# Gated linear attention followed by a squared-ReLU MoE layer: head-pair packing, one activation table and a new tracing order for the MoE

## The chip, the cores and the metric

The kernel runs on one core of one Trainium2 chip. The metric is the device time of one execution in microseconds (us). Engines are named as in the profile: PE (TensorE matmul), PEld (TensorE weight load, overlapping PE), DVE (VectorE), ACT (ScalarE), POOL (GpSimd) and SP (SyncE, which issues the DMAs here). The kernel before took 289.77 us, the median of three runs (289.43 to 291.96).

## The reference, cut to what matters

```python
# q, k, v, alpha: (4 batches, 8 heads, 768 tokens, 48), float32; alpha in 0.8..1.0
for t in range(S):                                    # gated linear attention (GLA)
    state = alpha[:, :, t, :, None] * state + einsum('bhd,bhe->bhde', k[:, :, t], v[:, :, t])
    y[:, :, t] = einsum('bhd,bhde->bhe', q[:, :, t], state)
x = y.transpose(0, 2, 1, 3).reshape(3072, 384)
h = x @ w_in                                          # 384 x 2048 ("MoE", first half)
r = maximum(h, 0); g = r * r
out = g @ w_out                                       # 2048 x 384 ("MoE", second half)
```

Both kernels do the GLA in 24 chunks of 128 tokens. Within a chunk, the running product of alpha becomes exp of a cumulative sum of ln(alpha); q is multiplied by it, k is divided by it, and the rest is matmul. State passes from chunk to chunk. The MoE part of a group of tokens can run as soon as the group's chunks have left the GLA.

## The kernel before

This is one GLA chunk, cut to what the change and the argument touch.

```python
nc.scalar.activation(L, at, AF.Ln)                     # ACT: one table
nc.tensor.matmul(pm, lhsT=utri_b2, rhs=L, ...)         # PE: cumulative sum
for h in range(H):                                     # PE: 8 column sums
    nc.tensor.matmul(state_ps[0:D, HD + h:HD + h + 1], lhsT=L[:, h*D:(h+1)*D], rhs=ones_col, ...)
nc.scalar.activation(A, pm, AF.Exp)                    # ACT: another table
nc.scalar.activation(Ainv, pm, AF.Exp, scale=-1.0)
nc.scalar.copy(vb, vt)                                 # ACT
nc.vector.tensor_mul(qki[:, :, 0, 0:D], qt, A)         # DVE (cut)
nc.vector.tensor_mul(qki[:, :, 1, 0:D], kt, Ainv)      # DVE (cut)
for h in range(H):                                     # q and k of one head share a transpose
    nc.tensor.transpose(pqkT[:, h, :], qki[:, h, :, :], ident_bf)
nc.vector.tensor_copy(qT[0:D, :, :], pqkT[0:D, :, :])
nc.scalar.copy(kT[0:D, :, :], pqkT[64:64 + D, :, :])   # ACT, 1,024 elements a lane
for r in range(2):
    for hh in range(4):                                # scores, 128 rows of which 48 hold data
        nc.tensor.matmul(ps[:, hh, :], lhsT=kT[:, h, :], rhs=qT[:, h, :], ...)
    nc.vector.tensor_mul(sm[:, r*4:(r+1)*4, :], ps, utri_b.to_broadcast([P, 4, P]))
# ... output matmuls, xn, three transposes pxT, copy into xT_big (ACT), new state ...
```

The main loop places half of a 256-token MoE group (eight `ph` groups of three matmuls, then one `po` tile of sixteen) after every chunk. Half of the ReLUs are on ACT, half on DVE:

```python
gla_chunk(...)
if sc >= 2:
    moe1_slice(sc // 2 - 1, range(8 * i, 8 * i + 8))
if sc >= 6:
    moe2_slice(jj // 2, [jj % 2])
```

## Time and profile before

| what | before |
|---|---|
| median time, runs beside the kernel after | 289.6 us (289.11 to 291.96, 4 runs) |
| busy: PE, ACT, DVE, POOL | 220.0, 196.0, 170.5, 63.7 us of 287.6 |
| ACT table loads | 49, of 1,283 ns: 63 us |
| copy of a chunk's result into `xT_big`: sixth, last | 72.51, 259.56 us |

The copy into `xT_big` is the last step of a chunk's GLA output, and its start times are a clock for progress. From the sixth to the last they are (259.56 - 72.51) / 18 = 10.4 us apart.

From the profile page of the kernel before, these are the busy times, the forty slices of PE and ACT (each digit is tenths of a slice), and the shares of the chain that ended last:

```profile
PE 220.0 (76%) x2176; PEld 150.8 (52%) x2176; DVE 170.5 (59%) x382; ACT 196.0 (68%) x353; POOL 63.7 (22%) x108
PE   0334887867787868889869789988867989999884
ACT  2777677687879988773984878796765696633100
ACT 39%; PE 34%; issue 12%; DVE 9%; DMA 4%; SPq 1%; ACTq 0%; DVEq 0%
```

No engine is full on average, but the chain passes through ACT more often than through PE. From the groups of the same page (busy us, mean ns of one; then idle time of the engine before them and who ended it), the reason:

```profile
L145 DVE TENSOR_TENSOR qki_s<-qt,A 128x384 bf16<-128x384 f32 x24 | 13.3, 556 | 36.7 <-ACT A L135 36.7
L122 ACT ACT_TABLE_LOAD x24 | 30.8, 1283 | 0.4
L162 ACT COPY kT_s<-pqkT 48x1024 bf16<-48x1024 bf16 x24 | 24.2, 1009 | 9.4 <-DVE qT_s L161 9.0
L135 ACT ACT_TABLE_LOAD x21 | 26.9, 1283 | 0.3
```

DVE waited 36.7 us in all for the exp.

### The profile page before, as it was taken

How to read it: one execution, taken by the hardware profiler on the slowest of the kernel's cores; microseconds unless marked ns; L12 is line 12 of the kernel's file. 1: busy time of each engine (PE TensorE's matmuls, PEld its weight loads, DVE VectorE, ACT ScalarE, POOL GpSimd, SP SyncE). 2: the span in 40 equal slices, each digit the busy share in tenths (PEclk: the TensorE clock that was granted, in tenths of full speed). 3: DMA queues.
4: the chain of work that ended last, by engine and by line, in shares of the span. 5: the costliest groups of instructions: out<-in, count | busy, mean ns of one | idle time of the engine just before them, and what ended most of it. 6: DMA issues, size and time to landing. Idle time of an engine off the chain costs nothing.

```text
span 287.6 us, 5744 instructions
## 1 busy us (share of the span) xinstructions
PE 220.0 (76%) x2176; PEld 150.8 (52%) x2176; DVE 170.5 (59%) x382; ACT 196.0 (68%) x353; POOL 63.7 (22%) x108
## 2 busy tenths in 40 slices
PE   0334887867787868889869789988867989999884
PEld 0223654644454555656546556655545656666542
DVE  5145566768466666646567558656665757785500
ACT  2777677687879988773984878796765696633100
POOL 3000022222111223122123113221222212333300
PEclk9999998999979999797999999999979999999999
DMA  8999899600776395823633625653440200000111
GB/s 158 248 229 243 200 239 277 136 2 0 141 107 138 84 181 76 158 68 72 136 74 69 137 55 113 112 120 76 109 82 30 55 32 30 27 2 28 55 57 55
DMA packets 107036, 30.26 MB, mean 105 GB/s; under 512 B 100352, under 2 KB 105472, under 8 KB 107008
## 3 DMA queue, kind: packets, MB, share of 16 engines
q1 hardware_dynamic: 107008, 29.89, 48.3%
q8 instruction: 17, 0.28, 0.4%
q14 instruction: 11, 0.09, 0.1%
HBM read 25.17 MB, written 4.72 MB: 104 GB/s over the span
## 4 chain that ended last, share of the span: by engine, by line
ACT 39%; PE 34%; issue 12%; DVE 9%; DMA 4%; SPq 1%; ACTq 0%; DVEq 0%
PE ph L209 13%; PE po L228 11%; ACT L135 6%; ACT r L217 6%; ACT L122 5%; ACT L L122 4%; ACT A L135 4%; PE sc L170 3%; PE pqkT L158 3%; ACT kT_s L162 3%; ACT xT_big L189 2%; ACT state_b L201 2%; DMA w_out_f<-in_moe_w_out_dram 2%; DVE gT_big L218 2%; ACT vb L142 2%
## 5 line engine op out<-in xcount | busy, mean ns | idle before, releaser
L209 PE MATMUL ph<-xT_big,w_in_b 128*128 128x256 bf16 x576 | 94.4, 288 | 25.5 <-ACT r L217 14.7
L221 POOL TENSOR_TENSOR gT_big<-r 128x256 bf16<-128x256 bf16 x96 | 61.2, 637 | 206.2 <-DVE r L220 206.2
L228 PE MATMUL po<-w_out_b,gT_big 128*128 128x384 bf16 x384 | 85.8, 331 | 3.4 <-DVE ob L238 2.1
L209 PEld LDWEIGHTS <-w_in_b 128*128 128x128 bf16 x576 | 55.3, 102 | 44.6 <-issue 33.4
L217 ACT ACTIVATE r<-ph 128x256 bf16<-128x256 f32 x96 | 36.5, 380 | 35.6 <-PE ph L209 33.5
L218 DVE TENSOR_TENSOR gT_big<-r 128x256 bf16<-128x256 bf16 x96 | 31.7, 330 | 32.9 <-ACT r L217 30.1
L228 PEld LDWEIGHTS <-gT_big 128*128 128x128 bf16 x384 | 36.7, 99 | 19.8 <-issue 6.5
L220 DVE TENSOR_SCALAR r<-ph 128x256 bf16<-128x256 f32 x96 | 39.9, 415 | 4.6 <-PE ph L209 4.5
L172 DVE TENSOR_TENSOR sm<-sc,utri_b 128x512 bf16<-128x512 f32 x48 | 33.0, 688 | 14.4 <-PE sc L170 14.2
L145 DVE TENSOR_TENSOR qki_s<-qt,A 128x384 bf16<-128x384 f32 x24 | 13.3, 556 | 36.7 <-ACT A L135 36.7
L122 ACT ACT_TABLE_LOAD x24 | 30.8, 1283 | 0.4
L162 ACT COPY kT_s<-pqkT 48x1024 bf16<-48x1024 bf16 x24 | 24.2, 1009 | 9.4 <-DVE qT_s L161 9.0
L135 ACT ACT_TABLE_LOAD x21 | 26.9, 1283 | 0.3
L170 PEld LDWEIGHTS <-kT_s 128*128 128x128 bf16 x192 | 14.4, 104 | 23.2 <-ACT kT_s L162 11.8
L170 PE MATMUL sc<-qT_s,kT_s 128*128 128x128 bf16 x192 | 20.5, 234 | 7.0 <-ACT kT_s L162 5.6
L142 ACT CAST vb<-vt 128x384 bf16<-128x384 f32 x24 | 12.2, 509 | 17.0 <-PE sc L181 12.1
L161 DVE COPY qT_s<-pqkT 48x1024 bf16<-48x1024 bf16 x24 | 16.3, 679 | 7.1 <-PE pqkT L158 6.9
L158 PE MATMUL pqkT<-ident_bf,qki_s 128*128 128x128 bf16 x192 | 17.5, 243 | 3.8 <-DVE qki_s L150 3.8
L158 PEld LDWEIGHTS <-qki_s 128*128 128x128 bf16 x192 | 13.5, 109 | 9.0 <-DVE qki_s L150 8.3
L127 PE MATMUL state_ps<-ones_col,L 128*48 128x1 bf16 x192 | 9.6, 168 | 8.9 <-ACT L L122 8.7
L127 PEld LDWEIGHTS <-L 128*48 128x48 bf16 x192 | 7.4, 105 | 16.6 <-ACT L L122 8.7
L125 PE MATMUL pm<-L,utri_b_104 128*128 128x384 bf16 x24 | 8.6, 358 | 9.8 <-ACT L L122 9.8
(41 smaller groups left out, 218.9 us busy)
## 6 DMA issues: line engine op xcount, KB each, us to landing
qt<-in_q_dram SPq DMA_DIRECT2D x24, 192.0 KB, 3.5
kt<-in_k_dram SPq DMA_DIRECT2D x24, 192.0 KB, 4.0
vt<-in_v_dram SPq DMA_DIRECT2D x24, 192.0 KB, 4.3
at<-in_alpha_dram SPq DMA_DIRECT2D x24, 192.0 KB, 3.9
out_dram<-ob SPq DMA_DIRECT2D x24, 192.0 KB, 1.9
w_in_f<-in_moe_w_in_dram SPq DMA_DIRECT2D x4, 768.0 KB, 6.3
w_out_f<-in_moe_w_out_dram SPq DMA_DIRECT2D x4, 768.0 KB, 7.2
```

Of the source, the lines that this page charges most:

```text
L122: nc.scalar.activation(L, at, AF.Ln)
L135: nc.scalar.activation(A, pm, AF.Exp)
L158: nc.tensor.transpose(pqkT[:, h, :], qki[:, h, :, :], ident_bf)
L162: nc.scalar.copy(kT[0:D, :, :], pqkT[64:64 + D, :, :])
L170: nc.tensor.matmul(ps[:, hh, :], lhsT=kT[:, h, :], rhs=qT[:, h, :], start=True, stop=True)
L172: nc.vector.tensor_mul(sm[:, r * 4:(r + 1) * 4, :], ps, utri_b.to_broadcast([P, 4, P]))
L209: nc.tensor.matmul(ph, lhsT=w_in_b[:, j, f * P:(f + 1) * P], rhs=xT_big[:, j, t0:t0 + TG], start=(j == 0), stop=(j == KT - 1),)
L217: nc.scalar.activation(r, ph, AF.Relu)
L218: nc.vector.tensor_mul(gT_big[:, f, g % 3, :], r, r)
L220: nc.vector.tensor_single_scalar(r, ph, 0.0, ALU.max)
L221: nc.gpsimd.tensor_mul(gT_big[:, f, g % 3, :], r, r)
L228: nc.tensor.matmul(po, lhsT=gT_big[:, kf, g % 3, tt * P:(tt + 1) * P], rhs=w_out_b[:, kf, :], start=(kf == 0), stop=(kf == FT - 1),)
```

## The change

Its intent is to relieve ACT, to halve the count of small PE and DVE operations by treating two heads at once, and to run the MoE in wider groups. The diff is long; this is its core.

```diff
+    nc.scalar.preload_act_table_set("natural_log_exp_and_others")   # ln, exp, relu, copy in one set
...
-        for h in range(H):                                  # 8 column sums
+        for p in range(NP):                                 # 4, of two heads each
...
-        nc.scalar.copy(vb, vt)
+        nc.gpsimd.tensor_copy(vb, vt)
...
-        for h in range(H):
-            nc.tensor.transpose(pqkT[:, h, :], qki[:, h, :, :], ident_bf)
-        nc.vector.tensor_copy(qT[0:D, :, :], pqkT[0:D, :, :])
-        nc.scalar.copy(kT[0:D, :, :], pqkT[64:64 + D, :, :])
+        for p in range(NP):
+            nc.tensor.transpose(pT[:, p, :], qA[:, 2 * p:2 * p + 2, :], ident_bf)
+        for p in range(NP):
+            nc.tensor.transpose(pT[:, NP + p, :], kI[:, 2 * p:2 * p + 2, :], ident_bf)
+        nc.vector.tensor_copy(qkT, pT)
...
+        for p in range(NP):
+            for hh in range(2):                             # a head in rows 0..63 or 64..127
+                sl = slice(64 * hh, 64 * hh + 64)
+                nc.tensor.matmul(sc_ps[:, hh, p, :], lhsT=qkT[sl, NP + p, :],
+                                 rhs=qkT[sl, p, :], start=True, stop=True)
...
-        nc.vector.tensor_copy(xn, py)
+        nc.scalar.copy(xn, py[:, 0:HD])
...
-        nc.scalar.copy(xT_big[:, :, tok0:tok0 + P], pxT)
+        nc.vector.tensor_copy(xT_big[:, :, tok0:tok0 + P], pxT)
```

The state of two heads is kept as one block-diagonal tile. `pm`, `pT`, `py` and `pxT` share two rotating banks of PSUM (the memory that the matmuls write to). Chunks are loaded two ahead, and the weights are asked for earlier. All ReLUs go to ACT, up to 512 wide, with the squares alternating between DVE and POOL. The MoE groups and the order in which they are traced are new:

```diff
-    TG = 256
+    GN = [2, 2, 4, 4, 4, 4, 2, 2]           # chunks per MoE group
...
+        gla_chunk(s, pend.pop(s))
+        budget = total * max(0, s - 2) / (NT - 2)
+        while qi < len(moe_q) and moe_q[qi][0] <= s and spent < budget:
+            ...                             # trace the next MoE item; spent += its cost
```

The queue may only be drained as far as whole groups are ready, and the budget grows with the chunk number. A 512-token group becomes ready all at once, by which time the budget has run ahead. So its items are traced in one lump, behind chunks 8, 12, 16, 20 and 22 (counted from 0), and the last group after the loop.

## The prediction

> **What bounds the kernel now.** No engine is saturated. The busy table gives PE 220.0 us (76%), ACT 196.0 (68%), DVE 170.5 (59%), POOL 63.7 (22%); the chain of waits puts 39% on ACT, 34% on PE, 12% on issue. By stretches of 20 us, ACT holds 13 to 18 us busy of 20 through the middle, and a 128-token chunk takes about 10.4 us. What the other engines wait for is ACT: DVE waits 36.7 us for A (the exp), PE and its loads wait on kT_s and on relu. By groups, ACT spends 49 table loads of 1,283 ns = 63 us, two per chunk, because Ln and Exp come from different tables; kT_s costs 24.2 us, vb 12.2.
>
> **Removed, added, moved** (per chunk, durations from the groups by form):
> - ACT now about 8 us. One table set leaves one load (-2.6). kT_s (-1.0) and vb (-0.5) go to DVE and POOL; xn comes (+0.5), xT_big goes (-0.5). All relus come to ACT, 512 wide in the middle: the 256-wide one takes 0.38, so I estimate 0.59, 62 us in all against 36.5. ACT after: about 5.5.
> - DVE: r (0.42 x4) leaves; one 1,024-element copy of q and k together replaces qT_s at the same 0.68; pxT's copy is about 0.35. DVE about 5.3, from 7.
> - POOL: squares about 56 us, vb about 14: 70 in all, harmless.
> - PE: the MoE is unchanged in columns. 384 po matmuls at 0.16 pitch and 576 ph at 0.11 pitch (timeline) are 125 us, 5.2 per chunk. GLA is about 2.2 now. There are still eight transposes; scores run as four pairs of 64-row tiles (the Trainium skill, "TensorEngine Tiling (Array Packing)", Theoretical Speedup: up to 2x for a dimension up to 64; no trace here shows it yet), column sums, state and state reads halve in count. About 1.8 after: small.
>
> The table merge rests on the Trainium skill, "ScalarE: Activation LUTs", Table sets: one set holds both exp and ln. Its 1,283 ns is what the trace has.
>
> **On the critical path.** Steady state becomes PE-limited at 7.0 us per chunk if the interleaving were perfect. It won't be. The new budget loop traces the MoE in lumps: after chunks 8, 12, 16 and 20 some 16 ph groups and 2 to 4 po tiles come at once (up to 20 us of PE), before the next chunk's GLA, while the chunks between get nothing. Where the scheduler keeps trace order, GLA starves on PE during a lump and then runs alone, about 4.8 us per chunk (DVE 4.0 plus waits). Fully serial is 5.1 + 4.8 = 9.9; I take 8.5 to 8.8.
>
> Sum: the first six chunks stay bound by DMA (10 MB of inputs and weights at 200 to 270 GB/s, the page's slices): about 46 us. Eighteen chunks at 8.6: 155. Last 256 tokens plus leftover po: about 18, from 28 now. Exposed latency of the last chunk: about 6. Total about 225 us.
>
> **Prediction: 225 us, 8 in 10 between 200 and 254. Faster by over 2%: 0.95; within 2%: 0.03; slower: 0.02.**
>
> **What would show it.** One ACT_TABLE_LOAD. ACT busy near 130 us, DVE near 135, PE still highest near 190. Relu x128 at about 0.59 and 0.38. PE's chain share above ACT's. Slices: PE alternates between full and about half with a period of four chunks; PE waiting for DVE in the GLA-only stretches. First ph before 30 us.
>
> **What would make it wrong.** A scheduler that interleaves lumps well (below 205). Two rotating PSUM banks shared by four uses per chunk, or one score buffer, serialising GLA beyond 5 us (above 245). PE clock dropping in GLA-only stretches. Row-tiled matmuls not overlapping, or draining at each mode change. POOL squares of 512 colliding with DVE.

## More of the kernel before

The timeline of ACT in the kernel before, about one exp (start us, duration us), shows a table load ahead of the exp and another ahead of the next ln:

```profile
157.20 0.47 ACT L201 CAST state_b<-state_ps 48x384 bf16<-48x384 f32 x1
157.69 1.28 ACT L135 ACT_TABLE_LOAD   x1
158.98 0.49 ACT L135 ACTIVATE A<-pm 128x384 bf16<-128x384 f32 x1
...
160.29 1.28 ACT L122 ACT_TABLE_LOAD   x1
```

The Trainium skill, "ScalarE: Activation LUTs", section What ACT_TABLE_LOAD costs, gives about 1,283 ns for the load, as here. It adds about 1,380 ns of drain for each switch, which these lines do not show: `state_b` ends at 157.67, the load starts at 157.69, and the exp starts at 158.98.

## The result and the profile after

The kernel after took 237.75 us (237.08 to 238.66, 4 runs) against 289.6; ratio 0.8236, 95% interval 0.8199 to 0.8273: faster, inside the predicted range and 12.75 us above its centre.

From the page of the kernel after, the same lines as before, with POOL's slices in ACT's place:

```profile
PE 194.6 (82%) x1696; PEld 110.0 (47%) x1696; DVE 129.2 (55%) x253; ACT 129.4 (55%) x313; POOL 68.1 (29%) x101
PE   0055877887989979999989899998979979999974
POOL 4000333442002750005630006620016623320520
PE 57%; ACT 15%; DVE 14%; issue 6%; DMA 3%; POOL 2%; SPq 1%; ACTq 0%; DVEq 0%; POOLq 0%
L231 ACT ACTIVATE r<-ph 128x256 bf16<-128x256 f32 (+1 forms) x128 | 61.5, 492 | 24.0 <-PE ph L226 16.6
L165 DVE TENSOR_TENSOR qA_s<-qt,A 128x384 bf16<-128x384 f32 x24 | 15.8, 659 | 13.6 <-ACT A L153 13.6
```

The chain has moved from ACT (39% to 15%) to PE (34% to 57%). One table load is left. DVE's wait for the exp fell from 36.7 us to 13.6. POOL's digits show the new rhythm: bursts of squares every five or six slices. A table of the starts of the `xT_big` copies, read from the timelines, puts the time in place:

| kernel (span of the profiled run) | sixth copy | sixth to last | after the last |
|---|---|---|---|
| before (287.6) | 72.5 | 187.1 (10.4 per chunk) | 28.0 |
| after (235.9) | 57.1 | 159.7 (8.87 per chunk) | 19.1 |
| what the prediction's sum had (225) | 46 | 155 (8.6) | 24 |

The mean of 8.87 hides two kinds of chunk. After the sixth copy the intervals are 7.4, 6.2, 6.9, **14.0**, 6.4, 6.3, 7.1, **14.3**, 6.4, 6.7, 7.3, **14.5**, 6.4, 6.2, 7.3, **14.3**, 6.4, **15.8** us. The long ones are the lumps. The timeline of PE in the kernel after, inside a lump (start us, duration us, count):

```profile
148.62 1.55 PE L226 MATMUL ph<-xT_big,w_in_b 128*128 128x512 bf16 x6
150.01 0.33 PE L144 MATMUL misc<-L_s,utri_b 128*128 128x384 bf16 x1
150.24 1.49 PE L226 MATMUL ph<-xT_big,w_in_b 128*128 128x512 bf16 x6
151.56 0.17 PE L147 MATMUL misc<-ones_col,L_s 128*128 128x1 bf16 x1
151.73 1.55 PE L226 MATMUL ph<-xT_big,w_in_b 128*128 128x512 bf16 x6
153.12 0.22 PE L147 MATMUL misc<-ones_col,L_s 128*128 128x1 bf16 x3
```

The next chunk's first step, one matmul and four tiny ones at L144 and L147, is drawn out over 3.1 us because MoE matmuls stand between them. Its exp can start only after the last of them.

A lump is not all MoE, nor is the stretch behind it free of MoE. In the long interval from 111.4 to 125.7 us, PE ran 29 of the lump's 48 `ph` matmuls. In the three short intervals behind it (125.7 to 146.0 us) PE was still busy 18.80 of 20.3 us: 9.12 us with `po` and 5.31 us with `ph`. The scheduler thus moves a good part of a lump into the gaps of the GLA chunks.

Between lumps the GLA chunk shows as a chain. This is one chunk of the kernel after, its own links alone (the copy into `xT_big` is beside the chain):

```profile
125.92 0.49 ACT L153 ACTIVATE A<-misc 128x384 bf16<-128x384 f32 x1 [0.67 <-PE misc L147]
126.44 0.56 DVE L165 TENSOR_TENSOR qA_s<-qt,A 128x384 bf16<-128x384 f32 x1 [0.41 <-ACT A L153]
127.53 0.40 PE L172 MATMUL misc<-ident_bf,kI_s 128*128 128x128 bf16 x4
127.96 0.69 DVE L174 COPY qkT<-misc 128x1024 bf16<-128x1024 bf16 x1 [0.49 <-PE misc L172]
128.71 0.40 PE L180 MATMUL sc<-qkT 64*128 64x128 bf16 x8
129.15 1.29 DVE L184 TENSOR_TENSOR sm<-sc,utri_b 128x512 bf16<-128x512 f32 x2
130.77 0.34 PE L196 MATMUL misc<-vb,sm 128*128 128x48 bf16 x7
131.14 0.48 ACT L200 CAST xn<-misc 128x384 bf16<-128x384 f32 x1 [0.91 <-PE misc L196]
131.68 0.34 PE L203 MATMUL misc<-ident_bf,xn 128*128 128x128 bf16 x3
131.85 0.33 PE L144 MATMUL misc<-L_s,utri_b 128*128 128x384 bf16 x1
132.06 0.36 DVE L204 COPY xT_big<-misc 128x384 bf16<-128x384 bf16 x1 [1.61 <-PE misc L203]
132.36 0.49 ACT L153 ACTIVATE A<-misc 128x384 bf16<-128x384 f32 x1 [0.73 <-PE misc L147]
132.88 0.56 DVE L165 TENSOR_TENSOR qA_s<-qt,A 128x384 bf16<-128x384 f32 x1 [0.47 <-ACT A L153]
```

From exp to exp is 132.36 - 125.92 = 6.44 us, and the next chunk's first matmul (L144) runs only behind this one's transposes (L203). DVE's own work in it is 4.0 us (0.56 + 0.55 + 0.69 + 0.56 + 1.29 + 0.36, with `kI_s` and the state, which are not shown). For the rest DVE waits, 0.49, 1.61 and 0.47 us (2.57 in all, as DVE's records overlap a little), and the other lines show for what: for transposes on PE, for the output on PE with its copy on ACT and its transposes, and for the next cumulative sum and exp.

A small loss is also to be seen. Two lines of the timeline of the kernel after:

```profile
119.43 1.04 POOL L233 TENSOR_TENSOR gT_1538<-r 128x512 bf16<-128x512 bf16 x1 [0.51 <-ACT r L231]
119.77 1.12 DVE L165 TENSOR_TENSOR qA_s<-qt,A 128x384 bf16<-128x384 f32 x1 [0.57 <-ACT A L153]
```

The multiplication for q takes 1.12 us here, against 0.56 us in the chunk above, where no POOL square ran. The Trainium skill, "SBUF — State Buffer", section Who interferes with whom, says that a DVE instruction with two SBUF inputs contends with a GpSimd instruction that reads SBUF; the trace agrees. It is a small term: the mean over 24 chunks rose from 556 to 659 ns, 24 x 0.103 = 2.5 us in all.

### The profile page after: what moved, and what is told of

It reads as the page before. It is cut to its first block, busy times and chain, and to the rows that moved or that the text cites. A ratio compares the mean times of both kernels' runs of the same rounds, so it can differ in the third digit from the quotient of the medians.

```text
span 235.9 us, 4581 instructions
## 1 busy us (share of the span) xinstructions
PE 194.6 (82%) x1696; PEld 110.0 (47%) x1696; DVE 129.2 (55%) x253; ACT 129.4 (55%) x313; POOL 68.1 (29%) x101
## 4 chain that ended last, share of the span: by engine, by line
PE 57%; ACT 15%; DVE 14%; issue 6%; DMA 3%; POOL 2%; SPq 1%; ACTq 0%; DVEq 0%; POOLq 0%
PE po L239 20%; PE ph L226 20%; ACT r L231 5%; DVE sm L184 4%; DVE qA_s L165 3%; ACT A L153 3%; PE sc L180 3%; PE misc L203 3%; PE misc L170 3%; DMA win_f<-in_moe_w_in_dram 3%; DVE qkT L174 3%; PE misc L172 2%; PE misc L196 2%; PE misc L144 2%; DVE ob L245 2%
## 5 line engine op out<-in xcount | busy, mean ns | idle before, releaser
L226 PE MATMUL ph<-xT_big,w_in_b 128*128 128x512 bf16 (+1 forms) x384 | 79.6, 328 | 1.5 <-ACT r L231 0.5
L231 ACT ACTIVATE r<-ph 128x256 bf16<-128x256 f32 (+1 forms) x128 | 61.5, 492 | 24.0 <-PE ph L226 16.6
L226 PEld LDWEIGHTS <-w_in_b 128*128 128x128 bf16 x384 | 35.5, 98 | 25.6 <-issue 8.1
L162 POOL CAST vb<-vt 128x384 bf16<-128x384 f32 x24 | 13.0, 542 | 77.0 <-DMA vt<-in_v_dram 31.4
L165 DVE TENSOR_TENSOR qA_s<-qt,A 128x384 bf16<-128x384 f32 x24 | 15.8, 659 | 13.6 <-ACT A L153 13.6
L174 DVE COPY qkT<-misc 128x1024 bf16<-128x1024 bf16 x24 | 16.5, 689 | 9.9 <-PE misc L172 9.9
L170 PE MATMUL misc<-ident_bf,qA_s 128*128 128x128 bf16 x96 | 10.1, 232 | 12.9 <-DVE qA_s L165 12.6
L196 PE MATMUL misc<-vb,sm 128*128 128x48 bf16 x192 | 13.1, 188 | 7.0 <-DVE sm L184 7.0
L153 ACT ACTIVATE A<-misc 128x384 bf16<-128x384 f32 x24 | 11.8, 490 | 11.7 <-PE misc L147 11.7
L196 PEld LDWEIGHTS <-sm 128*128 128x128 bf16 x192 | 9.4, 97 | 16.6 <-DVE sm L184 15.4
L239 PE MATMUL po<-w_out_b,gT_1095 128*128 128x384 bf16 x64 | 13.8, 325 | 0.8 <-DVE ob L245 0.5
L239 PE MATMUL po<-w_out_b,gT_1538 128*128 128x384 bf16 x64 | 13.5, 325 | 0.5 <-DVE ob L245 0.2
L141 ACT ACTIVATE L_s<-at 128x384 bf16<-128x384 f32 x24 | 12.6, 523 | 2.4 <-DMA at<-in_alpha_dram 2.0
L166 DVE TENSOR_TENSOR kI_s<-kt,Ainv 128x384 bf16<-128x384 f32 x24 | 13.2, 550 | 0.0
L247 ACT COPY ob<-po 128x384 f32<-128x384 f32 x12 | 5.7, 478 | 13.1 <-PE po L239 12.9
L239 PE MATMUL po<-w_out_b,gT_2031 128*128 128x384 bf16 x64 | 12.8, 325 | 0.1
```

Of the source, the lines that this page charges most:

```text
L153: nc.scalar.activation(A, pm[:, 0:HD].rearrange("p (h d) -> p h d", h=H), AF.Exp)
L162: nc.gpsimd.tensor_copy(vb, vt)
L165: nc.vector.tensor_mul(qA[:, :, 0:D], qt, A)
L166: nc.vector.tensor_mul(kI[:, :, 0:D], kt, Ainv)
L170: nc.tensor.transpose(pT[:, p, :], qA[:, 2 * p:2 * p + 2, :], ident_bf)
L174: nc.vector.tensor_copy(qkT, pT)
```

## The experiments

Twelve kernels ran. All gave correct results except the three marked as wrong.

### 1 and 2. Is it the table or the restructuring?

The theory was that the table loads alone held most of the gain; the rival was that the smaller and wider operations did. One kernel takes the preload alone, the other takes all but the preload.

```diff
 # e1_before_one_table: the kernel before
+    nc.scalar.preload_act_table_set("natural_log_exp_and_others")
 # e2_after_two_tables: the kernel after
-    nc.scalar.preload_act_table_set("natural_log_exp_and_others")
```

> The kernel before, with one line added: the table set that holds both exp and ln is loaded once at the start; nothing else changes. Theory A: ACT gates the kernel before, and the 49 table loads of 1,283 ns (63 us of ACT) are the largest single part of the gain; the chain of waits puts 31 us on them (10.9% of 287.6 us), so I expect 245 to 260 us, that is 30 to 45 of the 52 us that the whole change gained. Rival: the loads sit in ACT's idle time and the gain of the change came from the restructured GLA and the wider MoE groups: then at most 10 us, 280 or more. ACT busy should fall from 196 to about 134 us either way.

> The changed kernel without the line that preloads the joint table set, so ACT loads a table before Ln and before Exp in every chunk again. Theory A: the loads lie in the serial chain of a chunk (about 6.4 us from one xT copy to the next), so 24 chunks get up to 2.6 us longer: 265 to 290 us, and all or most of the gain is gone. Rival: ACT is at 55% now and has room: less than 3%, 238 to 245 us.

The preload alone took the time to 247.51 us (246.96 to 248.09; before 288.05; ratio 0.8595, 0.8552 to 0.8637). The restructuring alone took it to 277.29 us (276.43 to 278.16; ratio 0.9621, 0.9575 to 0.9668). Both fell in the bands of theory A. So one line was worth 40.5 us, more than the 31 us that the chain had put on the loads, and the long rest 10.8 us. Together they make 51.3, about what the whole change gave in its own rounds (51.9): the two add up. From the page of e1_before_one_table, its busy times and chain:

```profile
PE 208.9 (85%) x2176; PEld 145.0 (59%) x2176; DVE 171.3 (70%) x382; ACT 132.7 (54%) x305; POOL 64.0 (26%) x108
PE 50%; DVE 20%; ACT 16%; issue 8%; DMA 3%; SPq 1%; POOL 0%; DVEq 0%; ACTq 0%
```

With the loads away, ACT falls by 63 us and the chain already lies on PE. The copies of e1 tell more: sixth at 63.55 us, then 8.53 per chunk, then 28.1 after the last. Against it, the kernel after gains 6.5 us at the start and 9.0 at the end, and *loses* 6.1 in the middle (8.87 per chunk). What the restructured GLA saves in the middle, the long intervals of the lumps take back; experiment 4 tests this.

### 3, 4 and 5. Is it the order in which the MoE is traced?

The theory was that the lumps cost the middle its gain. Experiment 3 traces the MoE after everything else, experiment 4 spreads each group evenly over the chunks until the next group is ready, and experiment 5 repairs experiment 3.

```diff
 # e3_moe_last
-        budget = total * max(0, s - 2) / (NT - 2)
+        budget = 0
 # e4_moe_spread
-        budget = total * max(0, s - 2) / (NT - 2)
+        ready = sum(cost(it) for it in moe_q if it[0] <= s)
+        nxt = min([it[0] for it in moe_q if it[0] > s] or [NT])
+        budget = spent + (ready - spent) / max(1, nxt - s)
 # e5_moe_last_24_out_buffers: e3 and
-    opool = ctx.enter_context(tc.tile_pool(name="opool", bufs=3))
+    opool = ctx.enter_context(tc.tile_pool(name="opool", bufs=24))
```

> The changed kernel with the MoE budget at 0: all MoE work is traced after all GLA chunks, so the scheduler uses it only as filler. Theory B (the prediction's lumps): in each burst of 16 wide ph groups PE keeps the next chunk waiting; five intervals between xT copies are 14 to 15.8 us where the others are 6.2 to 7.3, some 38 us in all. With GLA first, the intervals become even, near 6.5 to 7.5 us, GLA ends near 185 us, leftover MoE follows: 210 to 225 us. Rival C: PE is the limit whatever the order (it shows nine tenths busy nearly everywhere), so the time stays within 2%, 233 to 242 us; the 14 us intervals vanish but the MoE left over at the end grows by as much.

> The changed kernel with the same MoE items, each group's 16 ph and 4 po spread evenly over the chunks until the next group becomes ready, instead of one lump. Theory B: bursts shorten, the 14 us intervals shrink to 8 or 9, 215 to 230 us. Rival C: within 2% of 237.7. If e3 gains and e4 does not, what counts is that GLA comes first, not that the MoE is even.

e3 took 242.06 us (241.66 to 242.73; ratio 0.8401, 0.8366 to 0.8436), slower than the kernel after and outside both bands. e4 took **224.66 us** (224.46 to 225.61; before 288.05; ratio 0.7802, 0.7767 to 0.7836), 13 us faster than the kernel after and in theory B's band, with intervals of 6.2 to 7.7 us in the whole middle and 12.8, 12.9 and 10.3 at the end, where the MoE work that is left sets the pace. The view of stretches of 20 us for e4 (busy us and count of PE, PEld, DVE, ACT and POOL; the granted clock, which is the share of TensorE's full clock; DMA share; GB/s):

```profile
100.00:120.00 20.00, 18.73 (x168) 9.01 (x166) 15.59 (x29) 14.91 (x36) 9.01 (x10) 1.00 0.48 98
120.00:140.00 20.00, 19.23 (x180) 9.96 (x179) 12.79 (x25) 11.81 (x27) 6.60 (x8) 1.00 0.94 194
140.00:160.00 20.00, 19.82 (x180) 10.24 (x178) 13.48 (x27) 13.98 (x34) 6.10 (x7) 1.00 0.34 82
160.00:180.00 20.00, 19.99 (x145) 10.59 (x144) 8.10 (x17) 10.04 (x21) 8.18 (x9) 1.00 0.08 30
```

and for the kernel after, two stretches of the same view:

```profile
120.00:140.00 20.00, 17.39 (x179) 9.50 (x176) 13.11 (x24) 8.39 (x25) 1.99 (x4) 1.00 0.66 145
140.00:160.00 20.00, 19.09 (x143) 9.33 (x142) 11.45 (x21) 13.15 (x27) 9.24 (x10) 1.00 0.38 84
```

PE (the first busy column) is 153.5 of 160 us from 60 to 220 us in e4, against 146.7 in the kernel after. Over the whole span PE is idle for 32.7 us in e4 and for 41.3 us in the kernel after (span less busy time), and busy for 190.2 us against 194.6. The two differences make up the 13 us; why the same 1,696 matmuls are busy for less was not followed. ACT and POOL are more even in e4 too: 11.8 and 14.0 us of ACT in the last two shared stretches, against 8.4 and 13.2.

Why did e3 go the other way? In it no `po` matmul ran for 67 us, from 78 to 145 us. The same view of e3, for the instructions of the tile `po` alone (PE, DVE, ACT):

```profile
80.00:100.00 20.00, 0.00 (x0) 0.00 (x0) 0.00 (x0) 0.84 0.59 116
100.00:120.00 20.00, 0.00 (x0) 0.00 (x0) 0.00 (x0) 0.99 0.66 129
120.00:140.00 20.00, 0.00 (x0) 0.00 (x0) 0.00 (x0) 0.74 0.64 128
```

The timeline has the third output buffer filled at 66.6 us and the first store of an output issued only at 137.99 us. Stores and chunk loads share the SP queue; tracing the MoE last puts every store behind every load in it, and the loads wait for the GLA to free their buffers. With three output buffers, `po` stops. The granted clock (the third number from the end) fell as well, to 0.74. But the GLA ended at 181.8 us, only 3.9 us later than in e5 below, so most of the loss is the `po` work that was left over. If that is the cause, more output buffers must cure it, with the order untouched:

> The run with the MoE traced last, with 24 output buffers instead of 3 and nothing else. In the run with 3, GLA did finish at 182 us instead of 217 with even intervals of 6.2 to 8.8 us, but no po matmul ran between 80 and 144 us: the first store stood behind the input loads in the DMA queue and left at 138 us, the three output buffers were full at 67 us, and the finished fourth tile kept the only po bank. Theory B': GLA first is right and the stores spoiled it; with a buffer for each store po fills the gaps: 208 to 222 us, po in every stretch from 60 us on. Rival C: the total is PE's work, the order does not matter: then it comes no lower than the spread version's 224.7, 224 to 236.

It took 225.42 us (224.92 to 226.95; before 288.48; ratio 0.7835, 0.7783 to 0.7887), and `po` is back. The same view of e5:

```profile
80.00:100.00 20.00, 6.88 (x33) 0.55 (x1) 0.48 (x1) 1.00 0.62 121
100.00:120.00 20.00, 5.08 (x24) 0.55 (x1) 0.00 (x0) 1.00 0.66 130
120.00:140.00 20.00, 8.55 (x40) 0.56 (x1) 0.48 (x1) 1.00 0.74 170
```

So two different orders without lumps, e4 and e5, both end at about 225 us. That the lumps cost about 12 us is shown by both; e3's loss came from its store queue. But e5 missed the band of theory B' and fell in rival C's. Its last copy came at 178.0 us against 197.4 in e4, and the time did not fall with it. Without lumps it no longer matters whether the GLA comes first: PE is busy for 191.7 of 223.2 us in e5 and 190.2 of 222.9 in e4.

### 6, 7 and 8. What paces the rest?

Experiment 6 asks whether the two rotating PSUM banks make the GLA serial: the output tile `py` moves into the score banks. Experiment 7 asks whether the weight loads delay the start: they are asked for behind the first chunks. Both build on e4. Experiment 8 builds on the kernel after and makes all groups 256 tokens, so that the lumps are half as large.

```diff
 # e6_spread_py_in_score_banks
-        py = ps_misc.tile([P, 512], FP32, name="misc")
+        py = ps_sc.tile([P, 2, NP, P], FP32, name="sc").rearrange("p a b c -> p (a b c)")
 # e7_spread_weights_behind: the loads of w_in leave the place ahead of the main loop
+        gla_chunk(s, pend.pop(s))
+        if s < 2:
+            load_w_in(2 * s, 4)
+            load_w_in(2 * s + 1, 4)
         if s < 4:
             load_w_out(s, 4)
-        gla_chunk(s, pend.pop(s))
 # e8_groups_of_256
-    GN = [2, 2, 4, 4, 4, 4, 2, 2]
+    GN = [2] * 12
```

> The spread version (224.7 us) with py moved from the two rotating PSUM banks to the score banks, so the two banks serve three uses per chunk and the next chunk's pm need not wait for this chunk's py. Theory D: the two banks make chunks strictly serial, at 6.2 to 7.2 us from xT to xT; with py out, intervals while GLA leads fall to 5 to 6 us and the time falls by 3 to 10 us, to 215 to 222. Rival C: PE is over 90% busy from 60 us on, so a shorter GLA chain only moves MoE work to the end: intervals shrink, time within 2% of 224.7. Also possible: py now holds the score banks, the next scores wait, and it gets slower, 226 to 235.

> The spread version with the weight loads and casts traced behind the GLA of chunks 0 to 3 instead of ahead of it. In the changed kernel ACT's second exp of chunk 0 stands behind a cast that waits for w_in until 10.2 us, and DVE too; the first xT comes at 17.2 us and the sixth at 56.5, where the prediction had 46. Theory E: that stall is the mis-sized term; the first xT comes at 11 to 12 us, the sixth at 49 to 52, the time falls by 4 to 6 us to about 219. Rival F: inputs and weights arrive at 240 GB/s until 47 us and that alone paces the first chunks: the first xT comes earlier, but the sixth by under 2 us, and the time stays at 222 to 227.

> The changed kernel with all MoE groups of 256 tokens, its own budget loop kept. Lumps are half as long, and half as many tokens have to be ready before the next ph can start, but relu costs 192 x 0.38 = 73 us of ACT instead of 61.5 and the weights are loaded twice as often. Theory B: the lump is what hurts, so smaller lumps gain: 222 to 231 us, with intervals alternating about 6.5 and 10 us. Rival G: the 512-wide groups are a part of the gain, so going back to 256 costs: 240 to 250 us.

e6 took 226.57 us (225.26 to 226.62; ratio 0.7855, 0.7806 to 0.7904): nothing gained, and the intervals stayed at 6.3 to 8.1. Theory D's band is missed; the time is in rival C's, but the intervals did not shrink as C expected. Experiment 12 shows a flaw of this test. e7 took 222.97 us (222.37 to 223.2; ratio 0.7734, 0.7681 to 0.7788), the fastest of all, but its interval overlaps that of e4 (0.7767 to 0.7836). The first copy came 2.8 us earlier (14.43 against 17.2), the sixth only 1.1 us earlier (55.39 against 56.45): theory E is missed, and both figures are in rival F's bands. F's reason, the arrival of the data, is put to the test in experiment 9. e8 took 236.54 us (235.59 to 236.73; ratio 0.8206, 0.8157 to 0.8254), about the kernel after and between the two bands. Its intervals alternate between 6.4 and 10 to 11 us, so lumps come twice as often at about half the surcharge. It also pays for width: 129.5 us of weight loads against 110.0, and 69.6 us of ReLU (192 at 384 ns) against 61.5. Smaller lumps are not the same as no lumps.

### 9. Are the first six chunks bound by DMA?

The prediction gave them 46 us because their inputs and the weights take that long to arrive. This kernel fetches only the first quarter of each weight matrix and casts it into all four pieces; casts and matmuls stay. The result is wrong.

```diff
-        t = wload.tile([P, KT, w], FP32, name="win_f", bufs=2)
-        nc.sync.dma_start(out=t, in_=w_in_r[:, :, sl])
+        if piece == 0:
+            first["in"] = wload.tile([P, KT, w], FP32, name="win_f", bufs=2)
+            nc.sync.dma_start(out=first["in"], in_=w_in_r[:, :, sl])
+        t = first["in"]                     # and the same for w_out
```

> The kernel after, but only the first quarter of each expert weight is fetched and cast into all four pieces (results wrong on purpose; the casts and all matmuls stay). Theory F (the DMA traffic of the first 50 us paces the first six chunks): the sixth transposed output comes at 38 to 47 us instead of 57.1 and the time falls by 8 to 15 us. Rival (the GLA chain, the casts on ACT or the first MoE lump pace the beginning): the sixth comes at 53 to 57 us and the time stays within 3 us of 237.75.

The sixth copy came at 53.3 us instead of 57.1, and the time was 234.45 us (234.06 to 234.78; before 288.21; ratio 0.8145, 0.8096 to 0.8194), 3.3 us below the kernel after. The place of the sixth copy is the rival's; the time misses the rival's band by 0.3 us and is far from the theory's. With 4.7 MB less to fetch, about 4 of the 11 us that the prediction missed at the start are accounted for. The rest is seen in the intervals: the first copy at 18.1 us, then 7.9, 6.8, 6.7, 6.6 and 7.2. The early GLA runs at its own chain's pace of about 7 us, even where the weights no longer queue ahead of its data. The view of waits of the kernel after agrees: between 17.4 and 57.1 us, from the first copy to the sixth, it puts no engine's wait down to a DMA.

### 10. Does the score matmul's speed rest on alternating row halves?

```diff
 # e10_spread_scores_apart: e4 and
-        for p in range(NP):
-            for hh in range(2):
+        for hh in range(2):
+            for p in range(NP):
```

> e4_moe_spread, but the score matmuls are issued so that neighbours use the same row half and not opposite halves. Theory (neighbours on opposite halves overlap, and PE work paces this version): the eight score matmuls take 0.55 to 0.6 us instead of 0.40 and the time rises from 224.7 to 226.5 to 230. Rival (the overlap is not needed or its gain is hidden): time 224 to 226.

It took 225.33 us (224.96 to 225.39; ratio 0.7822, 0.7782 to 0.7861), in the rival's band. One block of scores in the timeline of e4, then one of e10:

```profile
121.88 0.40 PE L180 MATMUL sc<-qkT 64*128 64x128 bf16 x8
```

```profile
122.50 0.41 PE L180 MATMUL sc<-qkT 64*128 64x128 bf16 x8
```

The single records in the trace are finer than these merged lines. In the kernel before, scores of 128 rows start 56 ns apart (the median). In e4 the eight start in pairs, 3 ns apart within a pair and 53 ns from one pair to the next: twice the rate. In e10 they start in pairs too, 13 ns apart within a pair and 43 ns to the next. So the changed order kept the rate. Whether neighbours in e10 really were on the same row half is not shown: the records do not name the half, and PE's order is not always the program's (the state matmuls, L208, are traced behind the transposes of L203 but run at 127.76 us in the kernel after, before those at 131.68). What forms the pairs in e10 stays open.

### 11 and 12. How fast is the GLA alone?

The prediction took 4.8 us per chunk for a GLA that runs alone. In these two kernels only the first group's MoE is computed, and its last output tile is stored for all others (wrong). The second one also moves `py` into the score banks, as e6 did.

```diff
+    moe_q = [it for it in moe_q if it[2] == 0]
...
+    for t in range(2, NT):
+        nc.sync.dma_start(out=out_r[t], in_=last_ob[0])
```

> The kernel after with the MoE of the first group alone (other output tiles get the last one's data, wrong on purpose), so that the GLA runs alone after about chunk ten. The prediction's step: 4.8 us per chunk. Theory D (the chain is serial through the two rotating PSUM banks and the one score buffer): 6 to 6.4 us per chunk, as the GLA-only stretches of the kernel after show.

> e11_gla_alone with the GLA output matmuls moved from the two rotating banks into the score banks. Theory D (the rotation of two banks makes the chain serial): the interval falls to about 5 us per chunk. Rival (the data dependencies themselves are the chain): the interval stays within 0.3 us of e11.

Both are single looks, state unknown: 187.23 and 193.27 us. The intervals are 7.1 us throughout in e11 and 7.1 to 7.5 in e12, slower than any theory had it. The view of stretches shows why they are not the measurement that was wanted. For e11:

```profile
30.00:35.00 5.00, 4.01 (x44) 2.60 (x41) 3.62 (x9) 4.25 (x12) 1.23 (x2) 1.00 1.09 276
100.00:140.00 40.00, 22.24 (x222) 15.25 (x223) 22.09 (x40) 14.05 (x40) 2.54 (x5) 0.50 0.60 122
```

The granted clock is 1.00 before about 41 us and 0.50 from about 66 us to the end. In the timeline four transposes last 0.61 us instead of 0.40 and the cumulative sum 0.53 instead of 0.33. With PE at half clock, its links of the chain are longer, and e11 and e12 cannot give the chain at full clock. An estimate can be had from e11's timeline. In its chunk from 120.63 to 127.72 us, the four passages of the chain through PE are 0.22, 0.21, 0.18 and 0.32 us longer than in the chunk of the kernel after that is shown above. Without these 0.93 us the lone chunk would take about 6.2 us, so that 4.8 us would be missed without any MoE. e12's interval is 0.3 us longer than e11's, so moving `py` does not shorten the chain, at half clock here or at full clock in e6. Two lines of e12's timeline show more:

```profile
121.60 0.50 PE L190 MATMUL sc<-sb,qkT 128*128 128x96 bf16 x4 [1.39 <-DVE sm L184]
123.33 0.53 PE L144 MATMUL misc<-L_s,utri_b 128*128 128x384 bf16 x1
```

The move brought a wait of its own: the reads of the state (L190), which in the kernel after run beside the masking of the scores (129.04 and 129.15 us), now wait until the masking has read the score banks. That makes up the 0.3 us: from the start of the masking to the copy `xn` is 2.26 us in e12 and 1.90 in e11. So e6 and e12 took one wait away and added another. For the banks they still tell something. With three users that take the two banks in turn, the next chunk's first matmul (L144) needed only the bank that the copy `qkT` had left by 119.54 us, and its input `L_s` was done by 118.24. PE stood idle for 1.39 us before 121.60, and L144 still came at 123.33, behind the transposes of `xn` at 123.04. What held it is then more likely its place in PE's order than the banks.

## Why the prediction was right or wrong

**ACT gates before; the table loads are the largest saving: right.** The preload alone is worth 40.5 us for 48 loads, 0.84 us each. The load lasts 1.283 us, so the time fell by about two thirds of the ACT time that was removed. The prediction rested this on the Trainium skill, "ScalarE: Activation LUTs", section Table sets, which says that one set holds both exp and ln; the trace agrees, with one load left.

**Busy times after: right.** ACT 129.4 us (130 predicted), DVE 129.2 (135), PE 194.6 (190), ReLU 0.599 and 0.384 us (0.59 and 0.38), first `ph` at 25.07 us (before 30).

**MoE lumps hold the GLA back: right, and shown.** That the chunks between get nothing was not right, as the next point says. The interval is 14.0 to 14.5 us at each lump, with a period of four chunks, and without lumps the kernel takes about 225 us (e4, e5).

**"GLA starves on PE during a lump and then runs alone, about 4.8 us per chunk (DVE 4.0 plus waits)": this is the step that was mis-sized.** DVE's part was right, 4.0 us. The waits were put at 0.8 us and are 6.44 - 4.0 = 2.4 us. Most of this is not handing over but work of PE and ACT that stands in series with DVE's: transposes, the output and its copy, the next cumulative sum and exp. The measured chunk takes 6.2 to 7.3 us between lumps, and about 6.2 us alone by the estimate from e11. Nor does it run alone there: leftover `po` and `ph` matmuls fill PE (18.80 of 20.3 us busy between two lumps), so the sign that PE would alternate between full and half did not come. The two errors partly cancel: 6.4 us instead of 4.8, but with MoE beneath it. That the mean, 8.87, came so near the predicted 8.6 is in part luck.

**The sum, term by term.** First six chunks: 46 predicted, 57.1 measured. Eighteen chunks: 155 and 159.7. The end: 24 and 19.1. The errors are +11.1, +4.7 and -4.9, which partly cancel (the measured terms add up to the profiled span, 235.9). The first term was mis-sized most: it was taken as the arrival time of the data, and behind the first chunk no wait is put down to a DMA. The kernel has 17.3 us until the first chunk's copy and five intervals of 8.0 after it. Taking three quarters of the weight traffic away brings back only 3.8 us (e9). The rest is again the chain of about 7 us per chunk.

**Its list of dangers.** Two banks or one score buffer making the GLA serial: not supported for the two banks, since moving one of the four users out gained nothing (e6, and e12 at half clock), though the move added a wait of its own; the one score buffer was not tested. A clock dip: not in the kernel after (1.0), but it does come when the MoE is removed (e11). Row-tiled matmuls not overlapping: they overlap in pairs, at twice the rate of the kernel before (56 ns for each matmul there, 56 ns for two here); a drain at each change of mode was not looked for. POOL colliding with DVE: real but small, 2.5 us of DVE time.

**What stays open.** The chain of a lone GLA chunk at full clock was not measured; 6.2 us is an estimate. That the next chunk's start waits for its place in PE's order is argued from the timelines of the kernel after and of e12; no run moved it. Why the first copy of the kernel after comes as late as 17.3 us was touched only by e7 (14.4), and little of that reached the sixth.

## What to carry to other kernels

Look first for repeated table loads on ACT when ln and exp alternate: here one line was worth four fifths of a rewrite's gain. When independent work is to fill the gaps of a serial chain, trace it in small even portions between the chain's steps: lumps of the same work cost about 12 us here, and a version with an even order (222.97 us, with weights loaded behind the first chunks) beats both kernels. If stores share a queue with loads, tracing work late also queues its stores late, so count the output buffers; and size a chain by the work of all engines that stand in series in it, not by its busiest engine.

## What the Trainium skill lacked or had wrong

- "ScalarE: Activation LUTs", What ACT_TABLE_LOAD costs: it gives about 1,380 ns of drain beside the 1,283 ns load, 2.66 us per switch. Here the load starts 0.02 us after the instruction before it ended and the next one starts as it ends, 1.31 us in all; removing 48 loads saved 0.84 us of the kernel's time each.
- "TensorE: Matmul & The Clock Gate", What's actually happening and HAM oscillation: the throttled state is said to come after an idle window of about 3.4 us, and the rule given is to have no longer gaps. In e11 the clock fell at about 41 us and stayed at 0.50 from about 66 us to the end, while no idle stretch of PE after the start was longer than 1.24 us; from 100 to 140 us PE was busy 22.24 of 40 us. So keeping to the rule was not enough. The page's "A second HAM failure mode" does tell of a clock that oscillates when PE idles briefly and often, without a figure for it. What in e11's stream lowered the clock was not tested.
- No page that was read says that stores traced late on a queue shared with loads can stop the engine that fills the output buffers: with three buffers, no output matmul ran for 67 us (e3), and 24 buffers gave 16.6 us back (e5).
